# Expert gathers, four slots of a whole token tile at a time: spread tokens kept in SBUF, one accumulated sum per tile

## The chip, the cores and the metric

One core of a Trainium2 chip runs the whole program. Its engines are TensorE (PE), VectorE (DVE), ScalarE (ACT), GpSimd (POOL) and SyncE (SP), each working through its own list of instructions in order, and they wait for each other by semaphores. The metric is the device time of one execution in microseconds. L12 stands for line 12 of the kernel before.

## The reference: what is computed

The input x has 2048 tokens of 448 channels. With xn its layer norm, the result is x + A(xn) + B(xn).

```python
xn = _layernorm(x)                                   # per token, over 448 channels
# A: short causal convolution of k (4 taps), times v, long causal convolution over 2048 tokens, times xn
kv = conv4(k, shift_k) * v
a  = xn * (irfft(rfft(kv, 4096) * rfft(ssm_k, 4096))[:2048] + kv * ssm_D)
# B: 16 heads, each picks 2 of 4096 experts for every token by two searches over 64 keys
s1, s2 = (xn @ w_q) split in two, each times its keys  # 64 scores each
top_e, top_s = best 2 of the 4 pairs of the two best of s1 and of s2
g   = softmax(top_s)
act = gelu(sum_d xn[n, d] * u[top_e, d])
out = sum over 16 heads x 2 of  g * act * v[top_e]
```

So each token asks for 32 rows of a table with 4096 rows, and a row of u and the row of v with the same number stand side by side in memory (896 values, 3584 bytes).

## The kernel before

**Tiles.** The tokens are 16 tiles T of 128. Each tile has 32 slots per token, NG = 32. For the experts a tile is cut into four groups j of 32 tokens, and each group of 32 tokens into 8 x 4 slots: partition p of a gather holds token 32 j + p % 32 and one of four slots of it. A *batch* b is (T, j, hf): four gathers of 128 rows each, so 128 batches and 512 gathers. Gathers are issued on POOL by e_gather (L508), into one of four buffers uv of 4 x 896 values.

**The way of a batch.** Its steps, with the function that writes each:

- e_spread (L521), PE: a product with a 0/1 matrix copies the 32 tokens of groups j and j + 1 to all 128 partitions, into the PSUM tile xr (one buffer of two banks).
- e_dots (L540, L547), DVE: for the first na of the four slots one product uv = xr * uv over na x 448 elements; for the others an operation that multiplies and sums as well (L547).
- e_gelu (L559, L563), ACT: sums each of the na products with an accumulating copy, then the gelu of the four sums.
- e_weigh (L574, L579), DVE: w = ge * gate, and where by_scale is false cc = fold * w, a 128 x 4 x 32 matrix with the weights at the places of the tokens. Where by_scale is true, e_scale (L589) makes cc on ACT in four scalings.
- e_values (L599, L602), PE: cc times the v half of the buffer, four column groups of PE side by side, summed over the two batches of j into the PSUM tile pv (one buffer). Its last product frees the uv buffer for the gathers four batches later.
- e_out (L612), ACT: copies pv to vs, once for each (T, j).
- e_fold (L621, L623): PE folds the four quarters of vs, and DVE adds the result to acc. e_store (L628) writes the tile out on SP.

**Stages.** First the weights: SP loads w_q, PE multiplies it by the keys (L303), and PE, ACT and DVE prepare them. Then the scores of every tile: s_turn, s_mm, s_split on PE and ACT, s_top on DVE (the eight best of 64 with MAX8, L407, and their places, L405), s_gate on ACT (L434 to L437), s_place on PE (L486), and s_put on ACT (L469, L470), which writes the table numbers idx and the gates gt that the gathers and e_weigh read. norm (L256 to L276) makes xn: DVE takes mean and variance with bn_stats, finds the inverse root by four Newton steps of small instructions, and ACT applies it. Then the long convolution in two halves of the channels (g = 0, 1): c_load (L639) loads k, v and ssm_k (hkv) for 56 channel groups, c_tap and c_prod (L658, L660, L668) do the four taps, c_in, c_spec, c_mul, c_inv, c_back, c_fin do the transforms on PE with tables fq that c_fm streams on SP (a ring of six), and c_gate (L798, L803) multiplies by xn and adds to acc. The expert batches run beside the scores and the convolution to the end.

**What sets the order.** No scheduler on the chip: the class Planner lists the instructions while the program is built. Each function is a stream of Op(engine, cost in us, function, what it waits for, ring of buffers that it takes from). The planner repeatedly starts the op that can begin earliest, with priorities from PRIO and from turn() and need(), which hold the convolution and the scores level with the gathers. The costs and LATE (what a landed gather is given on top) only shape the order; on the chip every instruction waits by semaphores alone. by_act(b) picks na by the loads that the planner sees; it is 4 as long as live["by_scale"] is true, which the kernel sets to false after the scores (L840). behind() (L494) adds to each gather a wait for the latest planned PE instruction that is BEHIND us old.

Of the kernel before, what the change touches and what calls it, by code (L numbers as in the profile page):

```python
# [10 lines left out]
F32 = mybir.dt.float32  # L11
# [7 lines left out]
P = 128  # L19
# [6 lines left out]
NBUF = 4  # L26
VERBOSE = False
BEHIND = 0.2
# [50 lines left out]
PRIO = {"c_back": 0.5, "c_delta": -0.1, "c_fin": 0.4, "c_fm": -0.4, "c_gate": -0.1, "c_hh": 0.5, "c_in": 0.5, "c_inv": 0.2, "c_mul": -0.2, "c_prod": -0.1, "c_spec": 0.3, "c_turn": 0.2, "c_zt": -0.5, "e_fold": -0.3, "e_gather": -0.5, "e_out": 0.5, "e_scale": -0.4, "e_spread": -0.5, "e_values": -0.5, "s_gate": 0.2, "s_put": -0.1, "s_top": 0.3, "s_turn": 0.1}  # L79
# [112 lines left out]
def parallel_kernel(ctx, tc, x, wq, kk, uv, hkv, const, fq, out):  # L192
# [57 lines left out]
    def norm(t0, t1):  # L250
        sl, n = slice(t0, t1), t1 - t0
        va, y0, y1 = (ap.tile([P, n], F32, name=f"n{i}_{t0}") for i in range(3))
        for t in range(t0, t1):
            def stats(t=t):
                st = rp.tile([P, 6], F32, tag="st", name="st")
                nc.vector.bn_stats(st, acc[:, t, :])  # L256
                nc.vector.bn_aggr(mv[:, t, :], st)
            yield Op("DVE", 0.78, stats, [("x", t0)])


        def guess():
            nc.vector.tensor_scalar(va, mv[:, sl, 1], 1e-5, None, op0=ALU.add)
            nc.vector.tensor_scalar(y1.bitcast(I32), va.bitcast(I32), 1, None, op0=ALU.logical_shift_right)
            nc.vector.tensor_scalar(y0.bitcast(I32), y1.bitcast(I32), -1.0, float(0x5F3759DF), op0=ALU.mult, op1=ALU.add)
        yield Op("DVE", 0.5, guess)
# [7 lines left out]
        yield Op("DVE", 0.17, lambda: nc.vector.scalar_tensor_tensor(nmr[:, sl], mv[:, sl, 0], -1.0, rstd[:, sl], op0=ALU.mult, op1=ALU.mult),  # L273
# [189 lines left out]
    def s_put(tiles):  # L463
        for T in tiles:
            last = T // 2 * 2 + 1 if T > 1 else T
            def put(T=T):
                pe, a = live.pop(("pe", T))
                pe = pe[:, a].rearrange("p j (w k) -> p j w k", w=2)
                nc.scalar.activation(idx[:, T].rearrange("p (j k) -> p j k", k=8), pe[:, :, 0], AF.Copy)  # L469
                nc.scalar.activation(gt[:, T].rearrange("p (j k) -> p j k", k=8), pe[:, :, 1], AF.Copy)  # L470
# [21 lines left out]
    order = [(T, j, hf) for T in range(NT) for j in range(4) for hf in range(2)]  # L492
# [9 lines left out]
    def e_gather():  # L502
        for b, (T, j, hf) in enumerate(order):
            for c in range(4):
                def go(b=b, T=T, g=8 * j + 4 * hf + c, c=c):
# [6 lines left out]
    def e_spread():  # L512
        for T in range(NT):
            for j in range(0, 4, 2):

                def go(T=T, j=j):
                    xr = ps_xr.tile([P, 2, 512], F32, tag="xr", name="xr")
                    for i in range(2):
                        live["xr", T, j + i] = xr[:, i, :]
                        b = slice(32 * (j + i), 32 * (j + i) + 32)  # L520
                        nc.tensor.matmul(xr[:, i, :D], rep[b].rearrange("p i s -> p (i s)"), xn[b, T, :], start=True, stop=True, tile_position=(32 * (j + i), 0))  # L521
                yield Op("PE", 1.15, go, [("xn", T)], key=("xr", T, j), rings=[(r_xr, ("dot", 8 * T + 2 * j + 3))], lag=0.2)
# [8 lines left out]
    def e_dots():  # L531
        for b, (T, j, hf) in enumerate(order):
# [3 lines left out]
            if na:  # L536
                def go(b=b, T=T, j=j, na=na, begin=begin):
                    begin()
                    u = live["uv", b][:, :na, :D]
                    nc.vector.tensor_mul(u, live["xr", T, j][:, None, :D].broadcast_to([P, na, D]), u)  # L540
                yield Op("DVE", 0.1 + 0.46 * na, go, [(("land", b, na - 1), LATE), ("xr", T, j - j % 2)], key=("mul", b), rings=[(r_act, ("ge", b))])
            for c in range(na, 4):
                def go(b=b, T=T, j=j, c=c, na=na, begin=begin):
# [3 lines left out]
                    nc.vector.scalar_tensor_tensor(u, live["xr", T, j][:, :D], 1.0, u, op0=ALU.mult, op1=ALU.mult,  # L547
                                                   accum_out=live["act", b][:, c:c + 1])
                yield Op("DVE", 0.63, go, [(("land", b, c), LATE), ("xr", T, j - j % 2)], key=("dot", b) if c == 3 else None,
# [4 lines left out]
    def e_gelu():  # L554
        for b in range(NB):
# [8 lines left out]
            yield Op("ACT", 0.25, ge, [("dot", b)], key=("ge", b), rings=[(r_ge, ("w", b))], lag=0.3)  # L564
# [5 lines left out]
    def e_weigh():  # L570
        for b, (T, j, hf) in enumerate(order):
            def go(b=b, T=T, j=j, hf=hf):
                w = live["w", b] = rp.tile([P, 4], F32, tag="w", name="w")
                nc.vector.tensor_mul(w, live.pop(("ge", b)), gt[:, T, 8 * j + 4 * hf:8 * j + 4 * hf + 4])  # L574
# [326 lines left out]
```

## Time and profile before

| | us |
|---|---|
| median of 3 runs (lowest, highest) | 831.16 (830.13, 832.6) |
| the profiled execution | 827.13 |
| its span | 825.4 |
| PE, DVE, ACT, POOL busy | 663.5, 704.4, 541.1, 492.2 |

The span runs from the first to the last instruction that the profiler saw; the profiled execution's own time has 1.7 us more around it. A line of the timeline gives start, duration, engine, line, operation, output and inputs, and in brackets how long the engine sat idle before it and what ended that. A line of the groups gives the line, engine, operation, output and inputs with shape and count, then busy time in us and the mean of one in ns, then the idle time just before such instructions and who ended it. A line of the windows gives from:to, length, busy us of PE, of PE's weight loads, of DVE, ACT and POOL with their counts, the granted clock of PE, the busy share of the DMA engines and GB/s. 16 DMA engines moved 278.5 MB, 234.9 MB of them for the gathers, a mean of 337 GB/s.

### The profile page before, as it was taken

The numbers are of one execution on the slowest core, as the hardware profiler recorded it, in microseconds if no ns is written. First come the engines' busy times: TensorE is split into PE (matmuls) and PEld (weight loads), VectorE is DVE, ScalarE is ACT, GpSimd is POOL, SyncE is SP. The second block draws the span as 40 slices with busy tenths as digits, with TensorE's granted clock in tenths as the row PEclk, the third lists the DMA queues.
The fourth block names the chain that finished last, engine by engine and source line by source line (L and its number), as shares of the span: only waits on it lengthen the run. The fifth ranks groups of instructions, "written<-read, shape, count | busy, mean of one in ns | idle before, by whom it ended". The sixth has DMA issues, their size and how long they took to land.

```text
span 825.4 us, 16762 instructions
## 1 busy us (share of the span) xinstructions
PE 663.5 (80%) x5052; PEld 386.1 (47%) x5052; DVE 704.4 (85%) x2633; ACT 541.1 (66%) x1862; POOL 492.2 (60%) x518
## 2 busy tenths in 40 slices
PE   6994999899799999755876778886567878787884
PEld 2463565565456665413543343444244533333561
DVE  4379999999999999955898999984799779999774
ACT  4431897677777767665785676765378656766852
POOL 0004666576667666662777766666365776776670
PEclk9997799999999999976989999899698999999998
DMA  9955898899989998999999999999899999999995
GB/s 333 381 211 175 293 329 306 305 334 329 320 309 351 331 323 300 336 340 365 387 351 323 396 373 383 366 350 387 286 396 350 313 402 399 383 395 396 330 377 187
DMA packets 80554, 278.53 MB, mean 337 GB/s; under 512 B 10320, under 2 KB 47568, under 8 KB 80464
## 3 DMA queue, kind: packets, MB, share of 16 engines
q0 software_dynamic: 40960, 234.91, 77.2%
q1 hardware_dynamic: 39360, 42.41, 15.3%
q8 instruction: 41, 0.67, 0.3%
q14 instruction: 49, 0.40, 0.1%
q10 hardware_dynamic: 144, 0.13, 0.1%
HBM read 273.75 MB, written 3.67 MB: 336 GB/s over the span
## 4 chain that ended last, share of the span: by engine, by line
DVE 62%; PE 15%; DMA 14%; ACT 4%; issue 4%; DVEq 0%; SPq 0%; POOL 0%; POOLq 0%; ACTq 0%
DVE uv L540 21%; DVE mi L405 11%; DVE mx L407 7%; DMA uv<-in_uv_dram,idx 7%; DMA x<-in_hkv_dram 6%; PE pw L303 3%; ACT uv L559 3%; DVE hh L738 3%; DVE hh L739 3%; DVE hh L743 2%; PE pv L602 2%; PE ps L693 2%; DVE tap L660 2%; DVE tap L658 2%; DVE uv L547 2%
## 5 line engine op out<-in xcount | busy, mean ns | idle before, releaser
L508 POOL DMA_INDIRECT uv<-in_uv_dram,idx x512 | 491.5, 960 | 313.5 <-issue 95.6
L559 ACT ACTIVATE uv<-uv 128x448 f32<-128x448 f32 x455 | 256.5, 565 | 118.5 <-DVE uv L540 118.2
L540 DVE TENSOR_TENSOR uv<-xr,uv 128x1792 f32<-128x1792 f32 (+2 forms) x128 | 232.0, 1812 | 27.1 <-DMA uv<-in_uv_dram,idx 21.2
L602 PE MATMUL pv<-uv,cc 128*32 128x448 f32 x1024 | 140.6, 592 | 0.0
L405 DVE FIND_INDEX8 mi<-mx,sc 128x8 uint32<-128x64 f32 x512 | 105.4, 240 | 0.0
L753 PE MATMUL psu<-hh,fm 128*128 128x224 f32 x264 | 70.9, 396 | 21.2 <-DVE hh L744 18.1
L559 ACT ACTIVATION_READ_ACCUMULATOR uv<-uv 128x1 f32 x455 | 85.1, 187 | 0.0
L599 PE MATMUL pv<-uv,cc 128*1 128x4 bf16 x128 | 21.5, 168 | 79.0 <-DVE cc L579 63.0
L363 PE MATMUL sc<-wh,xh 128*128 128x512 f32 x192 | 82.1, 428 | 1.6 <-DVE mi L405 1.6
L753 PEld LDWEIGHTS psu<-hh,fm 128*128 128x128 f32 x264 | 48.8, 204 | 66.2 <-ACT uv L559 31.7
L407 DVE MAX8 mx<-sc 128x8 f32<-128x64 f32 x512 | 74.5, 230 | 3.1 <-PE sc L367 2.9
L365 PE MATMUL sc<-wh,xl 128*128 128x512 f32 x192 | 76.2, 397 | 0.0
L364 PE MATMUL sc<-wl,xh 128*128 128x512 f32 x192 | 76.2, 397 | 0.0
L693 PE MATMUL ps<-cst,x 128*64 128x132 f32 x896 | 64.4, 303 | 10.2 <-DVE x L675 6.3
L693 PEld LDWEIGHTS ps<-cst,x 128*64 128x64 f32 x896 | 56.4, 151 | 32.4 <-DVE x L675 8.2
L599 PEld LDWEIGHTS <-cc 128*1 128x1 bf16 x128 | 10.2, 80 | 129.0 <-DVE cc L579 92.0
L721 PE MATMUL psf<-x,fm 128*128 128x448 f32 x132 | 62.0, 563 | 0.4 <-DVE hh L744 0.2
L589 ACT ACTIVATE cc<-rep,w 128x32 f32<-128x32 f32 x196 | 46.4, 307 | 12.7 <-DVE w L574 12.6
L363 PEld LDWEIGHTS sc<-wh,xh 128*128 128x128 f32 x192 | 36.9, 192 | 34.1 <-issue 18.0
L405 DVE MATCH_VALUE_LOAD mi<-mx,sc 128x8 f32 x512 | 45.9, 90 | 0.0
L521 PE MATMUL xr<-xn,rep 32*128 32x448 f32 x128 | 34.5, 617 | 13.4 <-DVE uv L540 11.9
L761 ACT ACTIVATE x<-psu 128x224 f32<-128x224 f32 (+1 forms) x66 | 23.4, 354 | 27.9 <-PE psu L753 27.6
(98 smaller groups left out, 1028.3 us busy)
## 6 DMA issues: line engine op xcount, KB each, us to landing
wq<-in_wq_dram SPq DMA_DIRECT2D x16, 896.0 KB, 13.4
x<-in_hkv_dram SPq DMA_DIRECT2D x14, 780.0 KB, 14.8
fm<-in_fq_dram SPq DMA_DIRECT2D x66, 128.0 KB, 6.6
uv<-in_uv_dram,idx POOLq DMA_INDIRECT x512
out_dram<-acc SPq DMA_DIRECT2D x32, 112.0 KB, 1.8
acc<-in_x_dram SPq DMA_DIRECT2D x1, 2240.0 KB
acc<-in_x_dram SPq DMA_DIRECT2D x1, 896.0 KB
cst<-in_const_dram SPq DMA_DIRECT2D x1, 540.0 KB
```

Source lines behind the costliest of these rows:

```text
L363: nc.tensor.matmul(sc, xh[:, c, :], wh[:, c, ns], start=(c == 0), stop=False)
L364: nc.tensor.matmul(sc, xh[:, c, :], wl[:, c, ns], start=False, stop=False)
L365: nc.tensor.matmul(sc, xl[:, c, :], wh[:, c, ns], start=False, stop=False)
L405: nc.vector.max_index(mi[:, T % 2, 8 * n + j, :], m, sc[:, 64 * j:64 * j + 64])
L407: nc.vector.max(m, sc[:, 64 * j:64 * j + 64])
L508: made = nc.gpsimd.indirect_dma_start(live["uv", b][:, c, :], None, uv, bass.IndirectOffsetOnAxis(ap=idx[:, T, g:g + 1], axis=0)).ins
L540: nc.vector.tensor_mul(u, live["xr", T, j][:, None, :D].broadcast_to([P, na, D]), u)
L559: nc.scalar.activation(u, u, AF.Copy, accum_out=live["act", b][:, c:c + 1])
L602: nc.tensor.matmul(pv[32 * c:32 * c + 32, :D], cc[:, c, :], buf[:, c, D:], start=(hf == 0), stop=(hf == 1), tile_position=(0, 32 * c))
L693: nc.tensor.matmul(ps[64 * i:64 * i + 64, w * j:w * j + w], src, f1[:, i, :], start=True, stop=True, tile_position=(0, 64 * i))
L721: nc.tensor.matmul(ps[:, :2 * HALF], live["fm", g, q][:, 0], x1[:, :, :, q, :].rearrange("p c t k -> p t c k"), start=True, stop=True)
L753: nc.tensor.matmul(ps[:, :HALF], fm[:, 1], hh[:, i], start=(i == 0), stop=(i == 1))
```

## The change

- **Batches.** order becomes (T, k), k from 0 to 7. A batch has slots 4 k to 4 k + 3 of every group, so slot c of it holds the tokens of group j = c. s_put writes idx and gt in that order.
- **Spread tokens.** e_spread's product goes to PSUM as before, and a new function e_keep copies it on ACT (128 x 896 at a time) to an SBUF tile xs of 4 x 448, of which there are two. e_dots multiplies uv by xs.
- **Sums.** e_values sums all eight batches of a tile into one pv; each of the four column groups is then a quarter of the tokens, and DVE adds pv to acc. e_out and the fold on PE go.
- **Gates.** e_weigh makes fg = fold * gate for two batches at a time (128 x 8 x 32) as soon as the gates are there, two buffers. cc = fg * ge is then one product on DVE (e_spots) or four scalings on ACT (e_scale).
- **Layer norm.** For tiles 2 to 15 the mean and the squares are summed on ACT by two accumulating passes over the tile; DVE keeps tiles 0 and 1 and all Newton steps.
- **Memory and order.** The scratch of GpSimd's descriptors is 8192 bytes per partition (16384 by default), the ring of fq tables five for six; BEHIND, LATE and PRIO have new values.

```diff
-BEHIND = 0.2
+FG = 2
+BEHIND = 0.5
...
+            def mean(t=t):
+                nc.scalar.activation(xn[:, t, :], acc[:, t, :], AF.Copy, scale=-1.0 / D, accum_out=mv[:, t, 0:1])
+            def squares(t=t):
+                nc.scalar.activation(xn[:, t, :], acc[:, t, :], AF.Square, bias=mv[:, t, 0:1], accum_out=mv[:, t, 1:2])
...
-            yield Op("DVE", 0.78, stats, [("x", t0)])
+            if t0 < 2:
+                yield Op("DVE", 0.78, stats, [("x", t0)])
+            else:
+                yield Op("ACT", 0.76, mean, [("x", t0)])
+                yield Op("ACT", 0.76, squares, key=("mv", t))
...
-    order = [(T, j, hf) for T in range(NT) for j in range(4) for hf in range(2)]
+    order = [(T, k) for T in range(NT) for k in range(8)]
...
+    def e_keep():
+        for T in range(NT):
+            for j in range(0, 4, 2):
+                def go(T=T, j=j):
+                    if j == 0:
+                        live["xs", T] = rp.tile([P, 4, D], F32, tag="xs", name="xs", bufs=2)
+                    nc.scalar.activation(live["xs", T][:, j:j + 2, :], live.pop(("xr", T, j))[:, :, :D], AF.Copy)
+                yield Op("ACT", 0.9, go, [("xr", T, j)], key=("xs", T, j))
...
-                    nc.vector.tensor_mul(u, live["xr", T, j][:, None, :D].broadcast_to([P, na, D]), u)
+                    nc.vector.tensor_mul(u, live["xs", T][:, :na, :], u)
...
-                    nc.vector.scalar_tensor_tensor(u, live["xr", T, j][:, :D], 1.0, u, op0=ALU.mult, op1=ALU.mult,
+                    nc.vector.scalar_tensor_tensor(u, live["xs", T][:, c, :], 1.0, u, op0=ALU.mult, op1=ALU.mult,
...
+        for T in range(NT):
+            for i in range(4):
+                def go(T=T, i=i):
+                    fg = live["fg", T, i] = rp.tile([P, 8, 32], F32, tag="fg", name="fg", bufs=FG)
+                    nc.vector.tensor_mul(fg, fold[:, None, :].broadcast_to([P, 8, 32]), gt[:, T, 8 * i:8 * i + 8][:, :, None].broadcast_to([P, 8, 32]))
+                yield Op("DVE", 0.42, go, [("idx", T)], key=("fg", T, i), rings=[(r_fg, ("cc", 8 * T + 2 * i + 1))])
+
+    def e_spots():
+        for b, (T, k) in enumerate(order):
             if not by_scale(b):
...
     def e_scale():
-        for b in range(NB):
+        for b, (T, k) in enumerate(order):
             if by_scale(b):
...
-                        nc.scalar.activation(cc[:, c, :], fold, AF.Copy, scale=w[:, c:c + 1])
+                        nc.scalar.activation(cc[:, c, :], live["fg", T, k // 2][:, k % 2 * 4 + c, :], AF.Copy, scale=ge[:, c:c + 1])
...
-                                     start=(hf == 0), stop=(hf == 1), tile_position=(0, 32 * c))
+                                     start=(k == 0), stop=(k == 7), tile_position=(0, 32 * c))
...
-            yield Op("DVE", 0.6, lambda T=T: nc.vector.tensor_add(acc[:, T, :], live["pf"][:, :D], acc[:, T, :]), [("pf", T)], key=("sum", T))
+            yield Op("DVE", 0.6, lambda T=T: nc.vector.tensor_add(acc[:, T, :], live.pop(("pv", T))[:, :D], acc[:, T, :]), [("v", 8 * T + 7)], key=("sum", T))
...
-    LATE = 1.0
+    LATE = 2.0
...
-    FM, HH, BC_LAST = 6, 3, GC // BC - 1
+    FM, HH, BC_LAST = 5, 3, GC // BC - 1
...
-    nc = bacc.Bacc("TRN2", target_bir_lowering=False, num_devices=1)
+    nc = bacc.Bacc("TRN2", target_bir_lowering=False, num_devices=1, dynamic_dma_scratch_size=8192)
```

by_scale, which both functions ask, is as before:

```python
    def by_scale(b):
        return live.setdefault(("sc", b), live["by_scale"])
```

More of the change, by code (lines that the diff above doesn't have):

```diff
@@ new lines, in e_spots, with put @@
+    def e_spots():
+        for b, (T, k) in enumerate(order):
+            if not by_scale(b):
+                def put(b=b, T=T, k=k):
+                    cc, ge = rp.tile([P, 4, 32], F32, tag="cc", name="cc", bufs=2), live.pop(("ge", b))
+                    live["cc", b] = cc
+                    nc.vector.tensor_mul(cc, live["fg", T, k // 2][:, k % 2 * 4:k % 2 * 4 + 4, :], ge[:, :, None].broadcast_to([P, 4, 32]))
+                yield Op("DVE", 0.28, put, [("ge", b), ("fg", T, k // 2)], key=("cc", b), rings=[(r_cc, ("v", b))])
```

81 lines of the change are left out of this document (30 added, 51 removed).

## The prediction

> **What bounds the kernel now.** I read the page first: busy shares, costliest groups, the chain's shares by engine.
>
> ```profile
> PE 663.5 (80%) x5052; PEld 386.1 (47%) x5052; DVE 704.4 (85%) x2633; ACT 541.1 (66%) x1862; POOL 492.2 (60%) x518
> L508 POOL DMA_INDIRECT uv<-in_uv_dram,idx x512 | 491.5, 960 | 313.5 <-issue 95.6
> DVE 62%; PE 15%; DMA 14%; ACT 4%; issue 4%; DVEq 0%; SPq 0%; POOL 0%; POOLq 0%; ACTq 0%
> ```
>
> By these DVE is the bound and POOL idles 40% of the time. The timeline of POOL alone says otherwise.
>
> ```profile
> 68.28 1.10 POOL L508 DMA_INDIRECT uv<-in_uv_dram,idx  x1 [66.97 <-ACT gt L470]
> 70.72 0.94 POOL L508 DMA_INDIRECT uv<-in_uv_dram,idx  x1 [1.34 <-PE sc L367]
> 71.97 0.95 POOL L508 DMA_INDIRECT uv<-in_uv_dram,idx  x1 [0.30 <-issue]
> ...
> 805.39 0.95 POOL L508 DMA_INDIRECT uv<-in_uv_dram,idx  x1 [0.30 <-issue]
> ```
>
> Back to back, a gather takes 0.95 us and 0.30 us pass before the next with nothing to wait for: a pitch of 1.25. So 511 pitches make 639 of the 737 us between the first gather (68.28) and the last (805.39). Of the 313.5 idle us, 67 lie ahead of the first gather and 511 x 0.30 = 153 belong to the pitch; 93 are real waits. The kernel is 68 us of start, 737 of gathers and 20 of tail, and its gather stream has 13% of slack. By stage, with the groups and the busy times of the two windows:
>
> ```profile
> L508 POOL DMA_INDIRECT uv<-in_uv_dram,idx x196 | 185.4, 946 | 163.3 <-ACT gt L470 67.0 <-issue 36.7 <-PE pv L602 33.1
> L508 POOL DMA_INDIRECT uv<-in_uv_dram,idx x316 | 306.1, 969 | 150.3 <-issue 58.9 <-ACT uv L559 28.5 <-PE ps L693 10.4
> 69.00:350.00 281.00, 250.03 (x1483) 154.69 (x1483) 275.98 (x1631) 205.83 (x757) 184.65 (x196) 0.95 0.91 318
> 350.00:806.00 456.00, 344.97 (x3156) 194.77 (x3151) 382.23 (x779) 304.03 (x1020) 305.80 (x316) 0.91 0.99 366
> ```
>
> In the stage of the scores (69 to 350) DVE is busy 276 of 281 us and POOL waits 163.3 - 67.0 - 195 x 0.30 = 38 us. In that of the convolution (350 to 806) DVE is busy 84%, and POOL waits 150.3 - 316 x 0.30 = 55 us, 31 of them in the two stretches where the chain of waits stands at the loads of hkv:
>
> ```profile
> 359.29 27.97 DMA x<-in_hkv_dram
> 558.82 24.47 DMA x<-in_hkv_dram
> ...
> L508 POOL DMA_INDIRECT uv<-in_uv_dram,idx x27 | 25.9, 958 | 25.0 <-issue 14.5 <-PE ps L693 4.8 <-DVE uv L547 2.6
> L508 POOL DMA_INDIRECT uv<-in_uv_dram,idx x29 | 28.2, 972 | 23.2 <-ACT uv L559 15.3 <-issue 5.5 <-PE psz L769 0.6
> ```
>
> The two groups are 350 to 400 (25.0 - 27 x 0.30 = 17) and 550 to 600 (23.2 - 29 x 0.30 = 14.5). So whatever lengthens a gather on POOL by more than this slack lengthens the kernel.
>
> **The main term: spread tokens in SBUF.** Before, the 128 products of L540 and the sums of L547 read one operand in PSUM (xr) and one in SBUF (uv). Afterwards both lie in SBUF (xs, uv). The trace holds DVE instructions of either kind beside gathers:
>
> ```profile
> 428.79 0.69 DVE L660 TENSOR_TENSOR tap<-tap 128x512 f32<-128x512 f32 x1
> 431.87 0.69 DVE L658 TENSOR_TENSOR tap<-x,cst 128x512 f32<-128x512 f32 x1
> 432.60 1.42 DVE L660 TENSOR_TENSOR tap<-tap 128x512 f32<-128x512 f32 x2
> 437.86 0.70 DVE L658 TENSOR_TENSOR tap<-x,cst 128x512 f32<-128x512 f32 x1
> ...
> 428.86 1.44 POOL L508 DMA_INDIRECT uv<-in_uv_dram,idx  x1 [0.52 <-ACT vs L612]
> ...
> 432.06 1.32 POOL L508 DMA_INDIRECT uv<-in_uv_dram,idx  x1 [0.52 <-DVE uv L547]
> 433.68 1.15 POOL L508 DMA_INDIRECT uv<-in_uv_dram,idx  x1 [0.30 <-issue]
> 437.84 0.95 POOL L508 DMA_INDIRECT uv<-in_uv_dram,idx  x1 [0.30 <-issue]
> ...
> 121.85 2.03 DVE L540 TENSOR_TENSOR uv<-xr,uv 128x1792 f32<-128x1792 f32 x1
> 122.52 0.94 POOL L508 DMA_INDIRECT uv<-in_uv_dram,idx  x1 [1.30 <-PE pv L602]
> ```
>
> L660 and L658 have both inputs in SBUF. The gather at 428.86 takes 1.44 in place of 0.95: 0.49 more. If it needs something 0.13 us after its start (428.99) that L660 holds until 429.48, the stall is 0.49. The same 0.13 gives 431.87 + 0.69 - 432.19 = 0.37 for the second (measured 1.32 - 0.95 = 0.37), and 434.02 - 433.81 = 0.21 for the third (0.20). An operation that begins with the gather (437.86) does not stall it, and the product from PSUM at 121.85, which covers the gather at 122.52, stalls nothing. So a gather waits for the end of a DVE instruction with two SBUF inputs that was there first; I read the thing held as a port through which the gather fetches idx. POOL is in order, so every later gather is late by as much.
>
> The products become such instructions, and their mean is longer than the pitch:
>
> ```profile
> L540 DVE TENSOR_TENSOR uv<-xr,uv 128x1792 f32<-128x1792 f32 x88 | 177.8, 2020 | 11.1 <-DMA uv<-in_uv_dram,idx 9.4 <-PE xr L521 0.7 <-issue 0.3
> L540 DVE TENSOR_TENSOR uv<-xr,uv 128x1344 f32<-128x1344 f32 x24 | 37.3, 1552 | 11.3 <-DMA uv<-in_uv_dram,idx 11.3
> L547 DVE SCALAR_TENSOR_TENSOR uv<-xr,uv 128x448 f32<-128x448 f32 x57 | 34.4, 617 | 1.7 <-DMA uv<-in_uv_dram,idx 1.4
> L540 DVE TENSOR_TENSOR uv<-xr,uv 128x896 f32<-128x896 f32 x15 | 16.3, 1088 | 4.7 <-PE xr L521 2.4 <-issue 1.6 <-DMA uv<-in_uv_dram,idx 0.6
> ```
>
> The changed program's order has 68 products of four slots (51 of them in the scores), 29 of three, 25 of two, 6 of one, and 97 sums: 103 operations of 0.62. Take 0.12 off each for starts that the gather wins, and let the next gather's fetch fall anywhere in a pitch. Four slots hold 1.90, so each stops a gather for 1.90 - 0.625 = 1.275 (0.65 to 1.90): 68 x 1.275 = 87 us. Three slots: 1.43 - 0.625 = 0.81, x29 = 23. Two: 0.97 x 0.97 / 2.5 = 0.38, x25 = 9. One: 0.50 x 0.50 / 2.5 = 0.10, x103 = 10. The new gate products (below) add 2. For the short ones the rule can be tested on before: its 98 operations of 0.69 (42 of L660 and of L658, 14 of L668 by the loops) should give 0.57 x 0.57 / 2.5 x 98 = 13, while the page has 491.5 - 512 x 0.944 = 8. I scale the 44 us of the shorter ones by 0.65 to 29, and take 87 + 29 - 1 (removed w and cc) = **115 us**. Bounds: 49 where every product starts just after a fetch, 246 where just before one.
>
> Part is paid from the slack. In the scores the stalls are 51 x 1.275 = 65 against 38 of waits, so POOL takes the bound from DVE there; I let it use 30 of the 38. Of the other 55, 31 come from the loads of hkv, which stay: 15 used. Net 115 - 45 = **+70** (bounds: 49 - 93, below nothing, and 246).
>
> The Trainium skill, SBUF — State Buffer, section Who interferes with whom, has a remark against this: tensor_tensor was not seen to stall DMA, since it takes only the read side of the port shared with GpSimd, and descriptors need the write side (marked there as inferred). By that the term is 0. The gathers above disagree with it, by 0.49 us at most; the same section's rule that two SBUF inputs contend with a GpSimd read fits them.
>
> **DVE otherwise.**
>
> ```profile
> L579 DVE TENSOR_TENSOR cc<-rep,w 128x128 f32<-128x128 f32 x79 | 23.1, 292 | 4.4
> L574 DVE TENSOR_TENSOR w<-ge,gt 128x4 f32<-128x4 f32 x128 | 20.3, 158 | 6.3 <-ACT ge L563 6.1
> L256 DVE BATCH_NORM_STATS2 st<-acc 128x6 f32<-128x448 f32 x16 | 9.6, 602 | 2.9 <-DMA acc<-in_x_dram 2.9
> ```
>
> Removed: w (20), cc (23), 14 layer-norm sums (14 x 0.60 = 8). Added: 64 gate products of 128x256, not in the trace, between 0.29 (cc, 128x128) and 0.69 (L660, 128x512); 0.42 by size, 27 us. Products 232 to 68 x 2.02 + 29 x 1.55 + 25 x 1.09 + 6 x 0.62 = 213; 40 more sums at 0.62 add 25. Net -18. Three more products stand ahead of the last index search (51 for 48): with free gathers the score stage would do 12 more in the same time. Worth 12 x 1.25 = 15 us if DVE stays its bound, 0 if POOL is. I take 0.
>
> **ACT.**
>
> ```profile
> L559 ACT ACTIVATE uv<-uv 128x448 f32<-128x448 f32 x455 | 256.5, 565 | 118.5 <-DVE uv L540 118.2
> L559 ACT ACTIVATION_READ_ACCUMULATOR uv<-uv 128x1 f32 x455 | 85.1, 187 | 0.0
> L589 ACT ACTIVATE cc<-rep,w 128x32 f32<-128x32 f32 x196 | 46.4, 307 | 12.7 <-DVE w L574 12.6
> L612 ACT ACTIVATE vs<-pv 128x448 f32<-128x448 f32 x64 | 33.9, 530 | 9.5 <-PE pv L602 9.5
> ```
>
> Every one of the 512 scalings (128 x 4) is on ACT in the new order, none on DVE: the loop of e_spots asks by_scale for all batches at its first step, while the flag is still true, and yields nothing. That is 316 more at 46.4 / 196 = 0.237: +75. The copies to xs, 32 of 128x896, lie between 0.53 and 1.06; 0.93, +30. The vs copies go: -34. Accumulations 455 to 415: -30. Layer-norm passes 28 x 0.75: +21. ACT goes from 541 to about 603, and in the convolution from 304 to some 350 of 456. I take 0, hidden in ACT's waits for L540 (118 us); bound: if the 77 batches left there each showed their four scalings, 77 x 0.95 = 73.
>
> **Smaller steps.** The 28 layer-norm passes stand ahead of the first tile's gates and index copy in ACT's order. Before, DVE's sums delayed that tile instead, and ACT sat idle for its gates:
>
> ```profile
> 65.21 0.21 ACT L434 ACTIVATE th<-dd 128x16 f32<-128x16 f32 x1 [7.42 <-DVE dd L429]
> ```
>
> Thirteen passes at 0.57, a spread copy and a few small ones come before the index copy, some 1 us more than that idle time: first gather near 69.5, **+1** (-3 to +5). One sum per tile: PE's first value product of a tile now waits for DVE's add, with PE's whole queue behind it; 16 times at most 0.62 plus a product of 2.02 = 42 us, taken at 0, because three other buffers are full meanwhile and 64 waits for the vs copy and the fold go. The next spread's first product waits for its ACT copy instead of DVE's last product, which comes earlier: 0. The gate product waits until ACT has scaled the batch three before, with DVE's next products behind it: 0, since the uv buffers ask the same of that batch one step later; at worst 64 x 0.95 = 61. The index and gate copies keep their 32 elements: 0. Five fq tables in place of six on SP's queue, the new priorities, and gathers tied to PE work 0.5 us back in place of 0.2: 0, at worst once more the 55 - 31 = 24 us of waits that are not at hkv.
>
> Half the scratch: the slowest landings the trace shows are 8.5 us, that is seven gathers in flight:
>
> ```profile
> 556.87 0.95 POOL L508 DMA_INDIRECT uv<-in_uv_dram,idx  x1 [0.30 <-issue]
> 565.32 1.56 DVE L540 TENSOR_TENSOR uv<-xr,uv 128x1344 f32<-128x1344 f32 x1 [1.02 <-DMA uv<-in_uv_dram,idx]
> ```
>
> Nothing if it still holds seven; if only four, 8.5 / 4 - 1.25 = 0.9 per gather at worst. I take 0. The Trainium skill, DMA: Bandwidth & Descriptors, sections Terms and The descriptor swizzle, gives 16 bytes and nine write descriptors per engine and transfer; 8192 bytes would then hold 56, an estimate that also gives 0.
>
> **Sum.** The profiled execution took 827.1 us (span 825.4), 4.0 under the median of the three timed runs, 831.2. 827.1 + 115 - 45 + 1 = 898; on the footing of the median, **902 us**.
>
> **Rivals.**
> 1. *Gathers are not held off by long products* (DVE gives way, or its order keeps them apart). For: the stalls in the rows are of 0.2 to 0.5 us, and none of 2 us was seen. Against: no DVE instruction in the rows gives way once begun. Then the 12 earlier gathers count, and most of the 9.5 us for which ACT waited to copy vs: 831 - 15 - 6 = 810, faster. It decides where the mean stall per batch stays under 45 / 128 = 0.35 us. Chance 0.09. The remark in SBUF — State Buffer of the Trainium skill, cited above, would give this.
> 2. *Starts fall just after fetches* and the slack takes nearly all: 831 + 49 - 45 + 1 = 836, a little slower or within the bound: 0.06.
> 3. *ACT becomes the bound* in the convolution, with its 73 on top: 975. For: the four scalings stand between every batch and its value product. Against: a quarter of ACT stays free. 0.07.
> 4. *The change does not do what it says*: the split of the scalings is dead code as shown; in the forecast already.
>
> **How the numbers follow.** Forecast 0.78: 902, and 847 to 957 for stalls between 60 and 170. The range, 836 to 960, takes in rival 2 and leaves out rivals 1 and 3, 0.16. A measurement of this kernel tells about 0.3% from no change. Faster 0.09; same 0.02, out of rival 2; slower 0.89.
>
> **What would show it.** Gathers of 1.5 to 2.9 us beside L562, mean near 1.17 in place of 0.96; POOL busy near 600; the score stage's end at 380 or later; DVE waiting for gathers in the scores; DMA under 320 GB/s. Wrong if gathers stay at 0.95 beside the products, or if POOL waits long for ACT.

## Result and profile after

The changed kernel takes **891.9 us** (median of 4 runs, 887.9 to 898.5), the kernel before 830.6 beside it (828.6 to 832.6): a ratio of 1.075, 95% interval 1.071 to 1.079. It is slower, by 61 us; 902 was forecast. The profiled execution took 890.5 (span 888.7). Below, a time is the median of all executions of a kernel, and a ratio leaves out those that came out over 1.5% above the kernel's fastest.

The page of the changed kernel: busy times, the DMA total, the chain's shares by engine, the group of the gathers.

```profile
PE 681.0 (77%) x4924; PEld 400.6 (45%) x4924; DVE 691.3 (78%) x2542; ACT 597.4 (67%) x2122; POOL 620.6 (70%) x518
DMA packets 80554, 278.52 MB, mean 313 GB/s; under 512 B 10320, under 2 KB 47568, under 8 KB 80464
...
DMA 37%; DVE 25%; PE 15%; issue 6%; POOL 6%; ACT 6%; SPq 4%; DVEq 0%; POOLq 0%; ACTq 0%
...
L522 POOL DMA_INDIRECT uv<-in_uv_dram,idx x512 | 619.9, 1211 | 250.8 <-issue 96.8
```

Against before, DVE does less, ACT 56 us more, and POOL 128 us more for the same 512 gathers: one takes 1.211 us in the mean in place of 0.960. The same bytes move, at 313 GB/s in place of 337. The chain has left DVE (62%, now 25%) for DMA (14%, now 37%, mostly the landing of gathers). Timelines of POOL and DVE, in the scores' stage, with the first and the last gather:

```profile
68.19 1.10 POOL L522 DMA_INDIRECT uv<-in_uv_dram,idx  x1 [66.89 <-ACT gt L483]
...
343.60 2.75 POOL L522 DMA_INDIRECT uv<-in_uv_dram,idx  x1 [0.30 <-issue]
346.65 0.95 POOL L522 DMA_INDIRECT uv<-in_uv_dram,idx  x1 [0.30 <-DVE mx L420]
...
350.40 2.30 POOL L522 DMA_INDIRECT uv<-in_uv_dram,idx  x1 [0.30 <-issue]
...
871.12 0.94 POOL L522 DMA_INDIRECT uv<-in_uv_dram,idx  x1 [0.30 <-issue]
...
343.50 2.02 DVE L562 TENSOR_TENSOR uv<-xs,uv 128x1792 f32<-128x1792 f32 x1 [2.13 <-DMA uv<-in_uv_dram,idx]
349.88 2.00 DVE L562 TENSOR_TENSOR uv<-xs,uv 128x1792 f32<-128x1792 f32 x1
```

The gather at 343.60 starts 0.10 us behind a product of four slots and ends at 346.35, 0.83 behind the product's end (345.52); the one at 350.40 ends at 352.70, 0.82 behind 351.88. An undisturbed gather has 0.95 - 0.13 = 0.82 left after the moment at which the prediction has it fetch its indices. So both stood still until the product was over.

I set up the same account for every kernel: **start** (the first gather's), **stretch** (busy time of the 512 gathers less 512 x 0.945), **waits** (POOL's idle time, less that ahead of the first gather, less 511 x 0.30) and **tail** (from the last gather's start to the span's end).

| us | start | stretch | waits | tail | span |
|---|---|---|---|---|---|
| before | 68.3 | 7.7 | 93.2 | 20.0 | 825.4 |
| after | 68.2 | 136.1 | 30.6 | 17.6 | 888.7 |
| difference | -0.1 | **+128.4** | **-62.6** | -2.4 | **+63.3** |
| predicted | +1 | +115 | -45 | 0 | +71 |

The group of the gathers in the two stages, cut at 350 us, shows where the waits went:

```profile
L522 POOL DMA_INDIRECT uv<-in_uv_dram,idx x179 | 224.1, 1252 | 124.7 <-ACT gt L483 66.9 <-issue 33.5 <-DVE mx L420 5.2
L522 POOL DMA_INDIRECT uv<-in_uv_dram,idx x334 | 396.7, 1188 | 126.5 <-issue 63.6 <-PE pv L630 14.4 <-ACT tap L662 10.1
```

Up to 350 us POOL waits 124.7 - 66.9 - 178 x 0.30 = 4 us (38 before), behind it 126.5 - 334 x 0.30 = 26 (55 before). POOL has become the bound: its own instructions, lengthened, leave it hardly a wait. DVE now waits for it, 101 us in all, and the last search of the scores comes 45 us later (the first two rows are after's, the last is before's):

```profile
DVE uv L562 <- DMA uv<-in_uv_dram,idx: 101.0, 64, 6.4
...
398.28 0.22 DVE L418 FIND_INDEX8 mi<-mx,sc 128x8 uint32<-128x64 f32 x1
```

```profile
353.16 0.22 DVE L405 FIND_INDEX8 mi<-mx,sc 128x8 uint32<-128x64 f32 x1
```

### The profile page after: what moved, and what is told of

It reads as the page before. It is cut to its first block, busy times and chain, and to the rows that moved or that the text cites. A ratio compares the mean times of both kernels' runs of the same rounds, so it can differ in the third digit from the quotient of the medians.

```text
span 888.7 us, 16617 instructions
## 1 busy us (share of the span) xinstructions
PE 681.0 (77%) x4924; PEld 400.6 (45%) x4924; DVE 691.3 (78%) x2542; ACT 597.4 (67%) x2122; POOL 620.6 (70%) x518
## 4 chain that ended last, share of the span: by engine, by line
DMA 37%; DVE 25%; PE 15%; issue 6%; POOL 6%; ACT 6%; SPq 4%; DVEq 0%; POOLq 0%; ACTq 0%
DMA uv<-in_uv_dram,idx 29%; DVE uv L562 9%; POOL uv L522 6%; SPq L652 4%; DMA x<-in_hkv_dram 4%; DVE mi L418 4%; PE psu L766 3%; ACT uv L581 3%; DVE mx L420 3%; PE pv L630 3%; PE psf L734 2%; DMA wq<-in_wq_dram 2%; DMA fm<-in_fq_dram 2%; PE pw L316 2%; DVE uv L569 2%
## 5 line engine op out<-in xcount | busy, mean ns | idle before, releaser
L522 POOL DMA_INDIRECT uv<-in_uv_dram,idx x512 | 619.9, 1211 | 250.8 <-issue 96.8
L581 ACT ACTIVATE uv<-uv 128x448 f32<-128x448 f32 x415 | 234.3, 566 | 170.3 <-DVE uv L562 168.9
L562 DVE TENSOR_TENSOR uv<-xs,uv 128x1792 f32<-128x1792 f32 (+3 forms) x128 | 213.3, 1668 | 101.9 <-DMA uv<-in_uv_dram,idx 101.0
L630 PE MATMUL pv<-uv,cc 128*32 128x448 f32 x1024 | 161.7, 614 | 0.0
L617 ACT ACTIVATE cc<-fg,ge 128x32 f32<-128x32 f32 x512 | 121.9, 311 | 1.9
L581 ACT ACTIVATION_READ_ACCUMULATOR uv<-uv 128x1 f32 x415 | 77.8, 187 | 0.0
L734 PE MATMUL psf<-x,fm 128*128 128x448 f32 x132 | 66.5, 598 | 7.4 <-DMA fm<-in_fq_dram 2.9
L569 DVE SCALAR_TENSOR_TENSOR uv<-xs,uv 128x448 f32<-128x448 f32 x97 | 59.7, 621 | 9.8 <-DMA uv<-in_uv_dram,idx 9.3
L630 PEld LDWEIGHTS pv<-uv,cc 128*32 128x32 f32 x1024 | 38.7, 114 | 17.7 <-issue 10.4
L802 PE MATMUL fin<-cst,zt 128*64 128x64 f32 x896 | 33.8, 234 | 15.4 <-ACT zt L789 15.3
```

The costliest lines, as they stand in the source:

```text
L522: made = nc.gpsimd.indirect_dma_start(live["uv", b][:, c, :], None, uv, bass.IndirectOffsetOnAxis(ap=idx[:, T, g:g + 1], axis=0)).ins
L562: nc.vector.tensor_mul(u, live["xs", T][:, :na, :], u)
L569: nc.vector.scalar_tensor_tensor(u, live["xs", T][:, c, :], 1.0, u, op0=ALU.mult, op1=ALU.mult, accum_out=live["act", b][:, c:c + 1])
L581: nc.scalar.activation(u, u, AF.Copy, accum_out=live["act", b][:, c:c + 1])
L617: nc.scalar.activation(cc[:, c, :], live["fg", T, k // 2][:, k % 2 * 4 + c, :], AF.Copy, scale=ge[:, c:c + 1])
L630: nc.tensor.matmul(pv[32 * c:32 * c + 32, :D], cc[:, c, :], buf[:, c, D:], start=(k == 0), stop=(k == 7), tile_position=(0, 32 * c))
```

## The experiments

The theory, **PORT**: a DVE instruction that reads two operands in SBUF holds off a gather's fetch of its indices, and the in-order POOL passes the delay on. That the held step is the fetch is a reading: the rows show a step about 0.13 us into the gather, and no run tells the fetch from another access to SBUF at that moment. Rivals: **ACT** (56 us more work there sets the end), **ORDER** (the copies to xs, or the new order, delay the batches), **RING** (half the scratch stalls the gathers).

### Spread in SBUF alone, and its control

`e1_before_sbuf` is the kernel before with half the scratch and the copies of the spread tokens to SBUF; its products read them there. `e2_before_copy_only` has the same scratch, copies and waits, but its products still read PSUM.

```diff
+                    nc.scalar.activation(xs, live["xr2", T, j][:, :, :D], AF.Copy)      # e1 and e2
...
-                    nc.vector.tensor_mul(u, live["xr", T, j][:, None, :D].broadcast_to([P, na, D]), u)
+                    nc.vector.tensor_mul(u, live["xs", T, j][:, None, :].broadcast_to([P, na, D]), u)      # e1 alone
...
```

Expected of e1:

> Theory PORT (a DVE instruction with two SBUF inputs holds off the next gather until it ends): before's program with one thing moved, the products read a copy of xr in SBUF, should lose nearly what the whole change lost. From the changed kernel's stalls per operation (four slots 1.25 us, three 0.95, two 0.42, one 0.07) its 88, 24, 15 and 58 such operations give 110 + 23 + 6 + 4 = 143 us of longer gathers (mean 0.96 to 1.23), less 50 to 60 of the 92 us of waits: 905 us (885 to 925). Rival ACT (the load of ACT made the change slow): 32 copies of 0.9 are 29 us of ACT, at most 840. Rival ORDER (batches of a whole tile, one sum per tile, the new plan): nothing of that is here, 831.

Expected of e2:

> The same copies to SBUF are made, but the products still read xr in PSUM; the copies are waited for and not used. PORT: gathers stay at 0.96 us, 831 us (822 to 840). Rival ACT or a rival by which the additional wait costs the time: as slow as the kernel before this one in the list.

Measured: e1 **901.0** us, ratio to before 1.083 (1.078 to 1.088); e2 **837.0**, 1.008 (1.004 to 1.011). First gather and group of the gathers, e1 and then e2:

```profile
70.45 1.10 POOL L508 DMA_INDIRECT uv<-in_uv_dram,idx  x1 [69.14 <-ACT gt L470]
...
L508 POOL DMA_INDIRECT uv<-in_uv_dram,idx x512 | 623.8, 1218 | 259.0 <-issue 95.8
```

```profile
67.87 1.10 POOL L508 DMA_INDIRECT uv<-in_uv_dram,idx  x1 [66.56 <-ACT gt L470]
...
L508 POOL DMA_INDIRECT uv<-in_uv_dram,idx x512 | 494.6, 966 | 318.2 <-issue 90.2
```

The two differ in where the products and the sums read, and so in what frees xr for the next spread (the copy in e1, the last product in e2), which should help e1 if anything. Stretch 140.0 against 10.8, waits 259.0 - 69.1 - 153.3 = 36.6 against 98.3: +129 and -62, almost exactly the split of the whole change. ORDER falls: the copies cost 6 us, and e1, which has none of the new order, loses as much as the whole change. (The new order alone was not run.) One edit of the change carries all of its loss.

### The hold by itself

`e5_bench` and `e9_bench_gaps` leave the computation out and run 16 gathers a stage beside a train of one kind of instruction, one execution each.

```diff
+        for _ in range(14):
+            nc.vector.tensor_mul(o, a, b)                # one stage; a and b in SBUF, 4 x 448 per partition
...
+        for c in range(NGA):
+            nc.gpsimd.indirect_dma_start(buf[:, c, :], None, uv, bass.IndirectOffsetOnAxis(ap=ii[:, c:c + 1], axis=0))
```

Expected of e5:

> The disputed hold measured by itself. This kernel leaves the whole computation of the reference out: in ten stages, one after the other, POOL issues the same 16 gathers of 128 rows of 896 floats, while VectorE (in the last stage ScalarE) runs a train of one kind of instruction without a gap: nothing; products of 4x448 with one input in PSUM; the same with both inputs in SBUF; one-slot products of 448 with both inputs in SBUF; one-slot products alternately with both inputs in SBUF and one in PSUM; copies SBUF to SBUF; tensor-scalar instructions; products from SBUF into PSUM; one-slot products with an accumulated sum; ScalarE copies. Theory PORT: gathers take 0.95 us beside nothing, beside the products with a PSUM input, beside instructions with one input and beside ScalarE; beside products with both inputs in SBUF each one that fetches its indices during such a product ends with it: a mean of 1.9 to 2.3 us beside products of 2.02 us, if the hold ends with each product, and one gather as long as the train (20 us or more) if a hold goes on through products that follow each other without a gap. Rival: not the ports but something else in the changed kernel holds the gathers (HBM, the ring): all stages at 0.95 us.

Expected of e9:

> A second measurement of the hold by itself; this kernel too leaves the whole computation out, and runs 16 gathers in each of eight stages beside a train on VectorE: nothing; one-slot products (both inputs in SBUF) on four slots in turn, so that each can start before the one ahead of it has ended; groups of four of these with a product that has an input in PSUM behind each group; products of two slots in turn; copies of 448 from SBUF to SBUF; copies of 1792 from SBUF to PSUM; copies of 1792 from PSUM to SBUF; batch-norm sums of 448. In the first measurement, products into one place, with 0.03 to 0.1 us between them, let one gather through at each boundary, and copies with a single SBUF input held the gathers too. Theory PORT, as refined: a hold ends only where the next instruction that takes both SBUF inputs (or copies at the doubled rate) has not begun yet. Products in turn that overlap then hold one gather for the whole train (30 us), or let one through only now and then; groups of four hold it for up to 2.2 us, a mean of 1.8 to 2.3 us; copies from or into PSUM and the sums leave 0.95 us. Rival: each hold ends at the end of its own instruction; products in turn then give 1.0 us as in the first measurement, and so do groups of four.

Group of the gathers in windows of e5: beside products with a PSUM input (27 to 47 us), products from SBUF (57 to 86), copies from SBUF to SBUF (161 to 187), ScalarE copies (312 to 331); then three of the trains on DVE. The second and the third group include the stage's first gather, which starts together with the train; the table leaves it out.

```profile
L82 POOL DMA_INDIRECT buf<-in_uv_dram,ii x16 | 15.1, 945 | 8.9 <-issue 4.6 <-DVE po L76 4.3
L82 POOL DMA_INDIRECT buf<-in_uv_dram,ii x15 | 25.4, 1692 | 13.8 <-DVE po L76 9.5 <-issue 4.3
L82 POOL DMA_INDIRECT buf<-in_uv_dram,ii x13 | 24.2, 1864 | 13.1 <-DVE po L76 9.4 <-issue 3.7
L82 POOL DMA_INDIRECT buf<-in_uv_dram,ii x15 | 14.2, 946 | 4.6 <-issue 4.6
...
27.01 28.78 DVE L46 TENSOR_TENSOR o<-pr,b 128x1792 f32<-128x1792 f32 x14
...
56.25 28.86 DVE L49 TENSOR_TENSOR o<-a,b 128x1792 f32<-128x1792 f32 x14
...
160.02 27.09 DVE L59 COPY o<-a 128x1792 f32<-128x1792 f32 x24
```

| beside | one instruction | gather, mean beside the train, after the stage's first |
|---|---|---|
| nothing; products with a PSUM input; ScalarE copies | -, 2.02, 1.70 | 0.95 |
| products, both inputs in SBUF | 2.03 | 1.75 |
| the same into PSUM (11 gathers) | 2.04 | 1.73 |
| copies, tensor-scalar, SBUF to SBUF (one input) | 1.10 | 1.92 each |
| one-slot products in one place; with an accumulated sum (12 gathers) | 0.63 | 1.02, 1.03 |
| one-slot products, every other one with a PSUM input | 0.61 | 1.04 |
| e9: one-slot products on four slots in turn | 0.54 from one to the next | 1.30 |
| e9: groups of four of these, then one with a PSUM input | 0.62 | 1.17 |
| e9: two-slot products | 1.00 from one to the next | 1.70 |
| e9: copies of 448, SBUF to SBUF | 0.33 | 1.02 |
| e9: copies from SBUF to PSUM and PSUM to SBUF; batch-norm sums | - | 0.95 |

Three things follow. First, PORT holds with nothing else in the kernel: beside two SBUF inputs a gather takes 1.75 us, and 1.75 + 0.30 is 28.86 / 14 = 2.06, the step of the products: one gather gets through at each boundary. Second, the number of SBUF inputs is not the whole rule. Copies with one SBUF input, expected at 0.95, hold gathers for two copies each (1.95 + 0.30 = 2 x 27.09 / 24); they pass 1792 elements in 1.10 us, nearly twice the rate of a product (2.03). Copies from or to PSUM do not. The Trainium skill, SBUF — State Buffer, section Who interferes with whom, has both cases as contending with GpSimd for the port pair that it shares with VectorE; for copies and tensor-scalar, in the mode that uses two ports, it says that whoever issues first has the pair for the whole instruction. These rows agree, and show the same of products. Its remark that tensor_tensor was not seen to stall DMA does not carry over to gathers that read indices from SBUF: 1.75 against 0.945. Third, in these two kernels the hold ends with its own instruction. With products in turn, where each starts before the last is over (DVE's row below, 30.12 / 56 = 0.54), a gather takes 1.30, and 1.30 + 0.30 is three steps of 0.54: the refined theory (one hold for the train) expected 30 us and falls here. The rival was right in the mechanism; the 1.0 us that it gave was missed (1.30, and 1.17 in groups of four).

```profile
31.30 30.12 DVE L46 TENSOR_TENSOR o<-a,b 128x448 f32<-128x448 f32 x56
...
L75 POOL DMA_INDIRECT buf<-in_uv_dram,ii x15 | 19.5, 1301 | 4.6 <-issue 4.6
```

### Cutting the products

`e3_after_single` cuts the changed kernel's long products into one-slot products in a row, `e7_before_single` does so in the kernel before, `e6_after_apart` makes each slot's product an operation of its own that starts as its slot lands.

```diff
-                    nc.vector.tensor_mul(u, live["xs", T][:, :na, :], u)
+                    for c in range(na):
+                        nc.vector.tensor_mul(u[:, c, :], live["xs", T][:, c, :], u[:, c, :])      # e3
...
-                yield Op("DVE", 0.1 + 0.46 * na, go, [(("land", b, na - 1), LATE), ("xs", T, 0), ("xs", T, 2)], key=("mul", b), rings=[(r_act, ("ge", b))])
+                yield Op("DVE", 0.6, go, [(("land", b, c), LATE), ("xs", T, 0), ("xs", T, 2)], key=("mul", b) if c == na - 1 else None,      # e6, for each c < na
...
```

Expected of e3:

> The changed kernel, each product of four, three or two slots cut into products of one slot; order and operands are the same. PORT: no operation is longer than 0.62 us, so the 116 us that the longer ones cost the gathers fall to 415 x 0.07 = 30; 30 to 40 us of waits come back, since DVE has about 43 us more to do (4 x 0.62 for 2.02). 840 us (820 to 860), gathers at 1.03. Rivals ACT and ORDER: no faster than 892, slower by up to DVE's 43 us.

Expected of e7:

> The control for the cut: the kernel before with its products, which have one input in PSUM, cut into one-slot products. PORT: the gathers stay at 0.95 to 0.97 us each; only the extra starts on VectorE count (some 22 us of its busy time in the changed kernel with the same cut, in a stage where its lateness already cost the gathers 38 us), 835 to 850 us. If short products are good or bad for the gathers whatever memory they read, their mean leaves 0.95 to 0.97 us.

Expected of e6:

> The changed kernel with its long products cut into one-slot products of 0.62 us, each an operation of its own that starts as its own slot lands, so that four of them no longer follow each other without a gap. With the cut alone the gathers were still 115 us longer than 0.945 us each, 93 of them beside the products; gathers of 2.2 to 3.0 us beside four products in a row. Theory PORT with a hold that goes on through products in a row: a product alone costs the gathers about 0.1 us, as the 97 accumulating ones did (10.0 us), so the stretch falls to some 60 us and the time to 815 to 850 us. PORT with a hold that ends with each product: no better than the cut alone, 860 to 880 us. Rival ACT: no change to 871 us either.

Measured: e3 **871.4** us, ratio to before 1.049 (1.042 to 1.056); e7 **846.3**, 1.022 (1.018 to 1.025); e6 **863.5**, 1.043 (1.039 to 1.047). The group of the gathers of e3, with one of its groups of four products and the gather beside it:

```profile
L522 POOL DMA_INDIRECT uv<-in_uv_dram,idx x512 | 599.5, 1171 | 251.7 <-issue 98.2
...
232.02 2.22 DVE L563 TENSOR_TENSOR uv<-xs,uv 128x448 f32<-128x448 f32 x4
...
232.11 2.96 POOL L522 DMA_INDIRECT uv<-in_uv_dram,idx  x1 [0.31 <-issue]
```

The same group of e7, and of e6:

```profile
L508 POOL DMA_INDIRECT uv<-in_uv_dram,idx x512 | 492.1, 961 | 330.4 <-issue 96.1
```

```profile
L522 POOL DMA_INDIRECT uv<-in_uv_dram,idx x512 | 553.2, 1080 | 281.9 <-issue 104.2
```

e7 came as expected: short products from PSUM leave the gathers at 0.96 us, and the cut costs 17 us in waits (330.4 - 67.3 - 153.3 = 110 against 93). e3 missed. I expected 840, with a stretch of some 50; it fell from 136.1 to 115.7 only. The gather at 232.11 shows why: it ends at 235.07, 0.83 behind the end of the fourth product (234.24), having passed three boundaries. By my count, with a group of four cut evenly, 16 of the 67 gathers that fetched ahead of the last product of a group got through at the first boundary, the others later. In e9's groups of four each gather got through at the first. The changed kernel itself has such cases too, about a dozen by the same kind of count. Its longest gather, of 4.97 us, starts in a gate product, passes that boundary and the one between two four-slot products, and ends 0.81 behind the second (147.77):

```profile
143.61 4.97 POOL L522 DMA_INDIRECT uv<-in_uv_dram,idx  x1 [0.30 <-issue]
...
143.48 0.41 DVE L598 TENSOR_TENSOR fg<-rep,gt 128x256 f32<-128x256 f32 x1
143.81 3.96 DVE L562 TENSOR_TENSOR uv<-xs,uv 128x1792 f32<-128x1792 f32 x2
```

So the prediction's rule, that a gather waits for the end of the instruction that was there first, is not the whole of it. **Why a boundary lets a gather through in e9 and mostly not in e3 stays open**; the products of e3 write over their own input and those of e9 do not, but no run separates that, and the gate product here, at whose end no gather got through, does not write over its input.

In e6, with products mostly apart, the stretch falls to 553.2 - 483.8 = 69.4, near the 60 expected of a hold that goes on through products in a row. The time did not follow, since waits rose from 30.6 to 281.9 - 67.6 - 153.3 = 61: of the 67 us that the stretch lost, 30 came back as waits (in the profiled execution, which took 856.0 us). By its time alone, 863.5, e6 lies outside the 815 to 850 of that form and inside the 860 to 880 of the other, so only the stretch speaks for it.

### Unloading ScalarE

`e8_after_spots` gives 79 batches' scalings back to VectorE, the split that the dead loop of e_spots loses.

```diff
-        return live.setdefault(("sc", b), live["by_scale"])
+        return b < 49
```

Expected:

> The changed kernel with the scaling of the fold by the gelu values on ScalarE for the first 49 batches only, and on VectorE in one product each for the other 79 (the split that the kernel before has, and that the changed kernel's loop order loses). ScalarE does 316 scalings of 0.31 us less, 98 us, VectorE 79 products of about 0.3 us more. PORT (POOL's gathers are the bound, ScalarE is not): 880 to 900 us. Rival ACT (ScalarE with 597 us busy sets the end): some 30 us or more faster, at most 860 us.

Measured: **912.6** us (903.0 to 920.8), ratio to before 1.104 (1.098 to 1.110), so 21 us over the changed kernel. Page:

```profile
PE 683.2 (76%) x4924; PEld 393.9 (44%) x4924; DVE 707.3 (78%) x2525; ACT 561.0 (62%) x1902; POOL 635.3 (70%) x518
...
L522 POOL DMA_INDIRECT uv<-in_uv_dram,idx x512 | 634.6, 1239 | 247.1 <-issue 98.0
L562 DVE TENSOR_TENSOR uv<-xs,uv 128x1792 f32<-128x1792 f32 (+2 forms) x128 | 236.0, 1844 | 102.3 <-DMA uv<-in_uv_dram,idx 101.5
```

ACT falls: 36 us less work on ScalarE (98 were expected) made nothing faster, and POOL's waits went from 30.6 to 247.1 - 67.8 - 153.3 = 26 only. PORT's 880 to 900 was missed too, by 13. The planner, seeing ScalarE lighter, gave the long products more slots: they take 236.0 us in place of 137.4 + 45.0 + 27.2 + 3.7 = 213.3 (groups further down; the 3.7 are six products of one slot), and the stretch is 634.6 - 483.8 = 150.8, 15 more. The profiled execution, 903.0, is the fastest of this kernel, so the rest of the 21 us is not in this profile. With the plan that follows from it, the dead loop saves time here.

### The other parts

`e4_before_half_scratch` changes the scratch alone. `e10_before_norm` has the layer-norm sums on ScalarE, `e11_before_gates` the gates placed early (with half the scratch), `e12_before_norm_gates` both, with half the scratch too. e11 and e12 fix the split of the scalings at b < 49, where before has it.

```diff
-    nc = bacc.Bacc("TRN2", target_bir_lowering=False, num_devices=1)
+    nc = bacc.Bacc("TRN2", target_bir_lowering=False, num_devices=1, dynamic_dma_scratch_size=8192)      # e4, e11, e12
...
+                yield Op("ACT", 0.76, mean, [("x", t0)])      # e10, e12
+                yield Op("ACT", 0.76, squares, key=("mv", t))
...
+                    nc.vector.tensor_mul(fg, fold[:, None, :].broadcast_to([P, 8, 32]), gt[:, T, 8 * j:8 * j + 8][:, :, None].broadcast_to([P, 8, 32]))      # e11, e12
```

Expected of e4:

> Before with half the scratch alone. PORT: 831 us within 3. Rival RING (half the scratch holds gathers up): part of the 61 us, at least 845.

Expected of e10:

> The kernel before with one part of the change alone: the layer-norm sums of tiles 2 to 15 on ScalarE. VectorE loses 14 x (0.602 + 0.182) = 11 us, all of it in the first 150 us, where its lateness costs the gathers some 10 of their 91 us of waits; ScalarE gains 28 passes. PORT has nothing to say here: no new instruction reads two SBUF inputs. Gathers stay at 0.96 us; 821 to 830 us, that is 0 to 10 us faster. A rival (ScalarE's passes delay the first tiles' indices): the first gather later than 69 us, and slower.

Expected of e11:

> The kernel before with half the scratch and one part of the change alone: gates placed early (64 products of 256 from gates and fold, both in SBUF, in place of 128 products of 4). VectorE gains 64 x 0.42 - 128 x 0.158 = 7 us, and one step leaves each batch's path from gelu to TensorE. PORT: 64 instructions of 0.42 us with two SBUF inputs hold some of the gathers for 0.2 to 0.3 us, 5 us in all at most; 828 to 838 us. Rival: the placing is itself what slows the changed kernel: 850 us or more.

Expected of e12:

> The kernel before with half the scratch, the sums on ScalarE and the gates placed early, that is the change without its spread in SBUF and without its new batches. PORT: the sum of the two parts, 820 to 835 us, gathers at 0.96 to 0.97 us. If the spread in SBUF is not the cause of the slowdown, this kernel is slower by tens of us, as the changed one is.

Measured, as ratios to before: e4 831.0 us, 1.001 (0.998 to 1.004); e10 838.7, **1.010** (1.007 to 1.013); e11 834.1, 1.002 (0.999 to 1.005); e12 845.8, **1.016** (1.011 to 1.021). RING falls with e4. The window from 69 to 350 us of e11, and its gathers from 350 on; then the last search and all gathers of e10:

```profile
69.00:350.00 281.00, 247.62 (x1505) 151.94 (x1504) 277.83 (x1527) 218.30 (x802) 199.74 (x211) 0.96 0.94 341
...
L508 POOL DMA_INDIRECT uv<-in_uv_dram,idx x302 | 294.5, 975 | 170.9 <-issue 56.9 <-ACT uv L559 47.8 <-ACT ge L563 7.9
```

```profile
344.37 0.25 DVE L416 FIND_INDEX8 mi<-mx,sc 128x8 uint32<-128x64 f32 x1
...
L519 POOL DMA_INDIRECT uv<-in_uv_dram,idx x512 | 492.2, 961 | 326.9 <-issue 88.8
```

e11 came as expected. It issues 211 gathers from 69 to 350 us where before issued 196, and ends no earlier: the gain is given back behind, where its waits are 170.9 - 302 x 0.30 = 80 us in place of 55. The scores themselves did not gain: their last search starts at 369.8 us, 17 later than before's. e10 missed. The 11 us taken off DVE ended the searches 9 us earlier (344.4 for 353.2), yet the waits rose to 326.9 - 67.7 - 153.3 = 106, and what else was late in its place I did not settle. The first gather, the sign of its rival, comes at 69.0 us, 0.7 later than before's: too little for the loss of 8. e12 missed too: its loss of 15 us is somewhat more than the two losses together (8 and 3), and its cause is open as well. But with gathers of 0.965 us it is far from the changed kernel, which differs from it by the spread and the batches. None of these versions beats the kernel before.

## Why the prediction was right

- **What bounds the kernel.** Right. The chain's shares named DVE, with 62%; the gather stream, with 13% of slack, decided: what lengthened the gathers by more than that slack lengthened the kernel.
- **Spread tokens in SBUF: +115.** Right in mechanism, but for the boundaries that a hold passes (above); measured +128. Groups of the products of the changed kernel:

```profile
L562 DVE TENSOR_TENSOR uv<-xs,uv 128x1792 f32<-128x1792 f32 x68 | 137.4, 2023 | 62.7 <-DMA uv<-in_uv_dram,idx 62.1
L569 DVE SCALAR_TENSOR_TENSOR uv<-xs,uv 128x448 f32<-128x448 f32 x97 | 59.7, 621 | 9.8 <-DMA uv<-in_uv_dram,idx 9.3
L562 DVE TENSOR_TENSOR uv<-xs,uv 128x1344 f32<-128x1344 f32 x29 | 45.0, 1553 | 24.8 <-DMA uv<-in_uv_dram,idx 24.6
L562 DVE TENSOR_TENSOR uv<-xs,uv 128x896 f32<-128x896 f32 x25 | 27.2, 1087 | 13.7 <-DMA uv<-in_uv_dram,idx 13.6
```

  Each stalled gather set beside the instruction that covers its fetch: 65 stalls beside the 68 four-slot products, 1.25 us each, 81 in all (predicted 1.275 and 87). The shorter ones: 28 for three slots, 7 for two, 8 for one and the sums, 5 for the gate products, 47 in all. The working had 44 and scaled it by 0.65 to 29, after the convolution's own operations. **That scaling is the term that failed**: unscaled, the sum is 130.
- **Paid from the slack: -45.** Mis-sized the other way: -63. The scores gave 34 of their 38 us (30 predicted), the rest 29 of 55 (15 predicted). I had taken the 31 at the loads of hkv to stay. The longest waits left are still near those loads, 9.8, 6.8 and 5.8 us beyond the pitch, but that is 22:

```profile
441.69 1.03 POOL L522 DMA_INDIRECT uv<-in_uv_dram,idx  x1 [10.13 <-ACT tap L662]
459.01 0.95 POOL L522 DMA_INDIRECT uv<-in_uv_dram,idx  x1 [7.11 <-PE pv L630]
640.89 0.94 POOL L522 DMA_INDIRECT uv<-in_uv_dram,idx  x1 [6.05 <-issue]
...
438.62 16.95 DMA x<-in_hkv_dram
649.45 19.27 DMA x<-in_hkv_dram
```

  Together the two errors nearly cancel, +13 against -18: +70 predicted, +66 measured. That the sum came so near is luck; the direction and the cost of the long products are not.
- **DVE otherwise, ACT.** DVE 691 busy (686 from the working), ACT 597 (603), a gate product 0.416 us (0.42), a copy to xs 0.899 (0.93). Both were taken at nothing; e8 bears it out for ACT, and DVE's part was not tried by itself.
- **Smaller steps.** First gather 68.2 (69.5 predicted, +1 for -0.1): the one step that was wrong in itself, and small. Half the scratch 0: shown by e4. One sum per tile, priorities, rings at 0: not tried one by one. The tail is 2.4 shorter.
- **Rivals.** Long products do hold gathers (rival 1 falls, by e1 and e5), starts do not all fall just after fetches (81 us for the long ones, 44 if they did), ACT is not the bound (e8), and the dead split is real but helps.
- **What would show it.** All six signs came: gathers of 1.5 to 2.9 us beside L562 (one took 4.97), mean 1.21, POOL busy 621, the score stage's end at 398, DVE waiting for gathers, 36 of the 101 us in the scores, and 313 GB/s.

## What to carry to other kernels

When a kernel lives on POOL's gathers, keep one input of every long VectorE product in PSUM: an SBUF copy of that operand, which looks like freedom, cost 64 us here. Before believing the chain's shares, count the instructions of a queue against its back-to-back pitch: an engine busy 60% of the time had 13% of slack. Making a step cheaper on an engine beside it gave nothing (norm, gates, scalings); in e11 what the scores' stage gained in gathers came back as waits later.

## What was not expected

- Copies and tensor-scalar instructions from SBUF to SBUF at the doubled rate (1.10 us for 1792 elements) hold gathers as two-input products do: 1.92 us a gather beside either.
- VectorE was not seen to be held in return: 14 products from SBUF beside gathers took 28.86 us in e5, and 14 with a PSUM input 28.78.
- A boundary between two products always let a gather through in the measurements by themselves, and inside e3's groups only 16 times in 67.
